# Three weight blocks of the output network decoded during attention, a ring of 25 slots, and a new order of attention's steps

## The chip, the cores and the metric

The kernel runs on one core of a Trainium2 chip. A core has five engines with queues of their own: PE (TensorE, matrix products), DVE (VectorE), ACT (ScalarE), POOL (GpSimd) and SP (SyncE, which here only issues transfers). PEld is PE's loading of stationary weights. The metric is device time in microseconds (us), less is better. The kernel before takes 501.9 us, the median of three runs from 501.25 to 503.02.

## What is computed

Three networks in a row, in fp32:

```python
scores = q @ k.T / 8                       # 4 batches x 12 heads, 448 x 448, causal
x = softmax(scores) @ v                    # -> 1792 tokens x 768
logits = x @ phi                           # 32 slots, 4 for each of 8 experts
d = softmax(logits, over tokens); c = softmax(logits, over slots)
slot_in = d.T @ x                          # 32 x 768
slot_out[e] = relu(slot_in[e] @ w1[e]) @ w2[e]      # 768 -> 1024 -> 768
y = c @ slot_out
h = y @ w_in                               # 768 -> 2048
out = (h * cos(h)) @ w_out                 # 2048 -> 768
```

The expert weights are 48 MB and must all be read once. w_in and w_out arrive as 64-bit words, 32 blocks of 768 KB, and are decoded to fp32 on the core.

## The kernel before, in words

**Attention** goes over 24 pairs of heads (4 batches x 6 pairs). The operations of a pair are small functions with short names: S0, S1, S2, Q3 are the score products of its four groups of rows (`qk_mm`, L334), sc and e the masked maximum on DVE and the exponential on ACT (`score`, L347), eps, rc and n the normalisation (L367 to L386, n on POOL unless the name ends in D or A), T0 and T1 the transposes of the probabilities for either head (`t_pair`, L399), ev0 to ev3 the copies of the transposed banks into pts (`ev_t`, L419), PV the product with v (`pv`, L424), evo the copy of x into xts (L436), X and evx the transposes of x back and their copies (L445, L452). Once in six pairs come the operations of a batch: phiA, phiB, ph4, ph5 (logits), dmax, dexp, dlg, dsum, dk, tk (the running softmax over tokens), u0, u1, ua0, ua1 (slot inputs).

The order is written out by hand: HEAD for steps 0 and 1, then ORDER once a step, TAIL from step 23. An entry ("T1", 1) in ORDER means T1 of the pair one step back. Every engine works through its own instructions in this order. `run_ops` (L634) walks it and puts loads between: when S0, S1, S2 and Q3 of a pair are out, q and k of the pair after next (`load_raw`), and in the later steps a piece of the expert weights too; after PV, the v of the pair after next.

**The ring.** `slot` (L238) gives out 26 buffers of 128 x 2048 words in turn. Attention holds seven (xk0, two for the probabilities, pts, xts, xk1, qk); the other 19 (`NPRE`, L544) take the first 19 pieces of w1 and w2, 1024 KB each, during attention. When attention is through with a slot (`FREE`, L631, seven conditions in order) the next piece goes there. xts holds x of four pairs at a time, and v of the odd pairs; x of the last pair lies in it, so its condition asks for the last X.

**The expert stream** (L822 to L862) takes the 48 pieces one after another (`next_piece`, L777). A piece that PE has used up frees its slot for a later one. Behind piece 36 the first three blocks of w_in and w_out (`NEW`) are loaded, behind piece 47 the next four. The first three are decoded (`decode`, L743) when pieces 42 to 44 are taken: an ACT pass (Prelu, L734), a DVE shift (L737) and a DVE shift with an or (L741). w_in blocks 0 and 1 go to fa, w_out block 0 to uacc.

**The output network** computes products in three fp32r terms (`back`, L949). A planner (from L1013) with costs and due times orders its operations; the first three blocks count as ready when it starts.

Of the kernel before, what the change touches and what calls it, by code (L numbers as in the profile page):

```python
# [27 lines left out]
NSLOT = 26  # L28
KP = 37
NEW = 3  # L30
# [47 lines left out]
ORDER = (  # L78
# [126 lines left out]
def moe_stack_kernel(ctx: ExitStack, tc: tile.TileContext, qk, v, cst, phi, w1, w2, w_in, w_out, out):  # L205
# [55 lines left out]
    ltr = lt[:, 0:112]  # L261
    dT = fixed.tile([128, NPB * NS], F32, name="dT")
# [35 lines left out]
    def load_piece():  # L298
        i = len(pieces)
        g, r = divmod(i, 24)  # L300
        t = slot(f"w{i}")
        if r < 12:
            SP.dma_start(t, w1[g, r // 6, r % 6])
        else:
            r -= 12
            SP.dma_start(t, w2[g, r // 4, r % 4])
        pieces.append(t)
# [13 lines left out]
    def XT(p):  # L321
        return xts[:, (p % 4) * 448:(p % 4 + 1) * 448]
# [301 lines left out]
    def all_ops():  # L624
# [7 lines left out]
            [("PV", last), ("X", last), ("phiA", 3), ("ph4", 3), ("ph5", 3)], [("u0", 3), ("PV", last - 1)], [("u1", 3), *SCORES])  # L632

    def run_ops():  # L634
# [3 lines left out]
        for op, i in all_ops():  # L638
            (PAIR if op in PAIR else BATCH)[op](i)
            done.add((op, i))  # L640
            while raws[0] < NPAIR and ok(raws[0] - 2, ("S0", "S1", "S2", "Q3")):
                load_raw(raws[0])
                raws[0] += 1
                if raws[0] > NPAIR - NPRE and len(pieces) < NPRE:
                    load_piece()
# [62 lines left out]
    def fwi(i):  # L708
        return ar[("fa", "fb")[i // 2 % 2]][:, 768 * (i % 2):768 * (i % 2) + 768]

    def it_f(j):
        kind, i = items[j]
        return fwi(i) if kind == "i" else (uacc, lt)[i % 2]
# [29 lines left out]
    def decode(j):  # L743
        dec_a(j)
        dec_l(j)
        dec_s(j)

    def up_part(c):
        f = (uacc, lt)[c % 2]
# [534 lines left out]
```

## Time and profile before

| | us |
|---|---|
| median of three runs | 501.9 |
| the profiled execution | 502.82 |
| its span, first to last instruction | 501.0 |
| PE, DVE, ACT, POOL busy | 478.5, 331.0, 307.8, 152.1 |

The page gives the busy time of each engine, the chain of waits that ended last and the costliest groups of instructions; other views give the same by stretches, lines and tiles, or in order of time. Times in the views count from the start of the span. A busy PE is not PE at its peak, since the ends of matmuls are modelled. The mean granted clock of TensorE is 0.990 of full speed.

### The profile page before, as it was taken

The page shows a single profiled execution, that of the slowest core. Times are in us where ns is not written, and L with a number is a line of the kernel's source. Part 1 is how long each engine was busy: PE and PEld are TensorE (multiplying, and loading weights), DVE is VectorE, ACT ScalarE, POOL GpSimd, SP SyncE. Part 2 cuts the span into 40 slices and gives each one's busy share as a digit, 9 for nine tenths or more (in the row PEclk, how much of TensorE's full clock was granted, in tenths as well). Part 3 has the DMA queues.
Part 4 walks back from the last instruction along what each step waited for, and adds up shares of the span by engine and source line. Part 5 has one row for each costly group of instructions (what it writes and reads, how often), then busy time and mean ns, then how long its engine had stood idle before and what let it go on. Part 6 is the DMA issues. An engine that isn't in the chain of part 4 may idle for free.

```text
span 501.0 us, 11371 instructions
## 1 busy us (share of the span) xinstructions
PE 478.5 (95%) x4329; PEld 346.2 (69%) x4329; DVE 331.0 (66%) x896; ACT 307.8 (61%) x736; POOL 152.1 (30%) x249
## 2 busy tenths in 40 slices
PE   7999999999998989879999999999999999999996
PEld 4766666666666433236877887877888888888885
DVE  4798889889885450022999888988877437336332
ACT  4898988999894110012888794858745555414452
POOL 1565555555542000000123122352421421213231
PEclk9999999999999899979999999999999999999999
DMA  6388878888867999999453545635110003023001
GB/s 204 106 285 310 292 287 295 287 294 295 289 248 259 378 423 420 419 418 418 137 178 125 190 158 217 227 108 178 61 61 2 0 2 113 14 105 118 31 1 63
DMA packets 23942, 100.38 MB, mean 200 GB/s; under 512 B 2768, under 2 KB 6352, under 8 KB 17744
## 3 DMA queue, kind: packets, MB, share of 16 engines
q1 hardware_dynamic: 23888, 99.66, 53.9%
q8 instruction: 34, 0.56, 0.5%
q14 instruction: 20, 0.16, 0.1%
HBM read 94.14 MB, written 5.51 MB: 199 GB/s over the span
## 4 chain that ended last, share of the span: by engine, by line
PE 55%; DMA 11%; DVE 3%; ACT 1%; issue 0%; SPq 0%; ACTq 0%
PE bank L954 13%; PE bank L956 13%; PE bank L955 13%; DMA w<-in_w_dram 11%; PE bank L923 3%; PE bank L984 2%; PE bank L983 2%; PE bank L985 2%; PE bank L832 2%; PE bank L884 1%; PE bank L433 1%; PE bank L542 1%; PE bank L897 1%; DVE zscr L931 1%; DVE zscr L939 0%; DVE lt L741 0%
## 5 line engine op out<-in xcount | busy, mean ns | idle before, releaser
L947 POOL TENSOR_TENSOR zg<-zscr,zg 128x512 fp32r<-128x512 f32 (+1 forms) x48 | 56.3, 1179 | 263.0 <-ACT zg L943 219.3
L954 PE MATMUL bank<-zg,zhl 128*128 128x512 f32 x282 | 112.4, 399 | 0.0
L956 PE MATMUL bank<-zg,zhl 128*128 128x512 f32 x282 | 110.2, 391 | 0.1
L955 PE MATMUL bank<-zg,zhl 128*128 128x512 f32 x282 | 110.1, 390 | 0.0
L362 ACT ACTIVATE p<-p,pst 128x192 f32<-128x192 f32 (+3 forms) x168 | 87.2, 521 | 15.3 <-DVE pst L360 14.7
L382 POOL TENSOR_SCALAR p<-p,pst 128x448 f32<-128x448 f32 (+3 forms) x123 | 66.8, 554 | 48.8 <-DVE pst L373 47.2
L931 DVE SCALAR_TENSOR_TENSOR zscr<-zscr,bank 128x512 f32<-128x512 int32 (+1 forms) x65 | 38.7, 610 | 37.4 <-ACT zscr L927 36.9
L954 PEld LDWEIGHTS bank<-zg,zhl 128*128 128x128 f32 x282 | 53.0, 188 | 12.7 <-issue 1.4
L956 PEld LDWEIGHTS bank<-zg,zhl 128*128 128x128 f32 x282 | 52.9, 188 | 11.8 <-DVE zg L947 0.4
L927 ACT ACTIVATE zscr<-bank,b_q 128x512 int32<-128x512 f32 (+1 forms) x65 | 39.4, 627 | 35.3 <-PE bank L923 33.7
L955 PEld LDWEIGHTS bank<-zg,zhl 128*128 128x128 f32 x282 | 53.1, 188 | 11.1
L344 PE MATMUL bank<-qk 64*128 64x320 f32 (+2 forms) x288 | 57.2, 467 | 0.0
L360 DVE CUSTOM_DVE_ANT_0 p<-bank,cs 128x448 f32<-128x448 f32 (+1 forms) x96 | 51.7, 553 | 5.8 <-PE bank L344 5.5
L935 ACT ACTIVATE zscr<-zscr,b_h 128x512 f32<-128x512 f32 (+1 forms) x65 | 41.6, 661 | 14.3 <-DVE zscr L931 13.3
L943 ACT ACTIVATE zg<-zscr 128x512 fp32r<-128x512 f32 (+1 forms) x65 | 36.4, 570 | 21.9 <-PE bank L955 11.4
L939 DVE TENSOR_TENSOR zscr<-bank,zscr 128x512 f32<-128x512 f32 (+1 forms) x65 | 39.0, 614 | 12.5 <-ACT zscr L935 12.5
L229 DVE COPY pts<-bank 128x512 f32<-128x512 f32 x47 | 32.1, 683 | 9.7 <-PE bank L389 9.0
L389 PE MATMUL bank<-cs,p 64*128 64x64 f32 (+1 forms) x768 | 34.7, 227 | 3.6 <-DVE p L384 2.1
L389 PEld LDWEIGHTS bank<-cs,p 64*128 64x128 f32 (+1 forms) x768 | 28.2, 133 | 12.6 <-ACT pts L227 7.1
L362 ACT ACTIVATION_READ_ACCUMULATOR p<-p,pst 128x1 f32 x168 | 31.8, 189 | 0.0
L227 ACT ACTIVATE pts<-bank 128x512 f32<-128x512 f32 x49 | 28.5, 582 | 2.3 <-PE bank L389 2.1
L734 ACT ACTIVATE zraw<-zraw 128x768 f32<-128x768 f32 x32 | 28.3, 902 | 1.6 <-DMA zraw<-in_w_out_dram 1.3
(167 smaller groups left out, 746.3 us busy)
## 6 DMA issues: line engine op xcount, KB each, us to landing
w<-in_w_dram SPq DMA_DIRECT2D x48, 1024.0 KB, 7.7
zraw<-in_w_in_dram SPq DMA_DIRECT2D x16, 768.0 KB, 4.8
zraw<-in_w_out_dram SPq DMA_DIRECT2D x16, 768.0 KB, 5.6
qk<-in_qk_dram SPq DMA_DIRECT2D x24, 480.0 KB, 3.5
xk<-in_v_dram SPq DMA_DIRECT2D x12, 256.0 KB, 3.8
out_dram<-zps SPq DMA_DIRECT2D x11, 256.0 KB, 2.1
xts<-in_v_dram SPq DMA_DIRECT2D x12, 128.0 KB, 4.0
lt<-in_v_dram SPq DMA_DIRECT2D x12, 128.0 KB, 4.1
```

The lines of the kernel that those rows point to most:

```text
L344: PE.matmul(sreg(j, c), lhsT=Q(p)[h, q0:q0 + 128], rhs=K(p)[h, 0:ln], start=True, stop=True)
L360: DVE.tensor_tensor_reduce(out=dst, in0=sb, in1=m, scale=-0.125, scalar=3.0e38, op0=ALU.add, op1=ALU.min, accum_out=st_[:, col:col + 1])
L362: return pr(f"exp{j}{c}")(lambda: ACT.activation(dst, dst, AF.Exp, bias=st_[:, col:col + 1], scale=-1.0, accum_out=st_[:, 8 + col:9 + col]))
L382: POOL.tensor_scalar(dst, dst, st_[:, 24 + col:25 + col], 0.0, op0=ALU.mult, op1=ALU.add)
L389: PE.transpose(out, src, by)
L927: ACT.activation(y_(s)[:, c].bitcast(I32), hb[:, c], AF.Identity, bias=b_q, scale=1.0 / (2.0 * math.pi))
L931: DVE.scalar_tensor_tensor(y_(s)[:, c], y_(s)[:, c].bitcast(I32), -2.0 * math.pi, hb[:, c], op0=ALU.mult, op1=ALU.add)
L935: ACT.activation(y_(s)[:, c], y_(s)[:, c], AF.Sin, bias=b_h, scale=1.0)
L947: eng.tensor_tensor(g_(s)[1][:, c], y_(s)[:, c], g_(s)[0][:, c].bitcast(F32), ALU.subtract)
L954: PE.matmul(o, lhsT=wh, rhs=gh, start=first, stop=False)
L955: PE.matmul(o, lhsT=wl, rhs=gh, start=False, stop=False)
L956: PE.matmul(o, lhsT=wh, rhs=gl, start=False, stop=last)
```

## The change

- The ring has 25 slots; 18 pieces are loaded during attention. A fixed tile, hold (128 x 2304 words), is new.
- The first three blocks of w_in and w_out are loaded into the last three of the 18 slots in steps 4 and 9, long before these take their pieces, and decoded into hold by passes that XTRA hangs behind certain operations of attention (d load, a the ACT pass, l the shift, s the shift with or). Their load and decode in the stream go. In hold they stay until the output network has used them; later hold stands in for the slot px.
- x of the last pair lies in the qk slot, and the conditions for the slots xts and qk in FREE change with it.
- HEAD, ORDER and TAIL are written anew. Norm n11 goes to DVE, n03 and n12 to POOL. The tail has one warm-up matmul (kwc) instead of seven.

The diff, with HEAD and TAIL cut to their first lines:

```diff
--- before.py
+++ after.py
@@ -25,7 +25,7 @@
 CH = ((0, 448), (128, 320), (256, 192))
 PO = (0, 448, 768)
 PW = 960
-NSLOT = 26
+NSLOT = 25
 KP = 37
 NEW = 3
 SEQ = ((0, 0, 2), (1, 0, 3), (2, 0, 4), (0, 2, 6), (1, 3, 8), (2, 4, 10), (0, 6, 13), (1, 8, 16), (2, 10, 16), (0, 13, 16), (3, 0, 16))
@@ -52,37 +52,41 @@
 LE = {1: 'D', 10: 'D', 11: 'D', 12: 'D', 13: 'D', 15: 'D', 16: 'D', 2: 'D', 23: 'D', 3: 'D', 30: 'D', 32: 'D', 39: 'D', 41: 'D', 42: 'D', 7: 'D', 9: 'D'}
 KW = 3
 HEAD = (
-    ("kwu", 1), ("S0", 0), ("sc00", 0), ("sc10", 0), ("S2", 0), ("e00", 0), ("Q3", 0), ("sc03", 0), ("S1", 0),
...
+    ("S0", 0), ("S1", 0), ("Q3", 0), ("S2", 0), ("sc00", 0), ("sc01", 0), ("sc10", 0), ("sc03", 0), ("kwu", 4),
...
+XTRA = {("e00", 4): ("d0",), ("n00", 3): ("d1",), ("sc00", 6): ("a0",), ("e01", 5): ("l0",), ("S2", 12): ("s0",),
+        ("S0", 9): ("d2",), ("n10", 10): ("a2",), ("rc1", 14): ("l2",), ("ev3D", 16): ("s2",), ("sc12", 15): ("a1",),
+        ("PV", 11): ("l1",), ("e03", 19): ("s1",)}
 TH = 2
 TT = 23
 TAIL = (
-    ("epsD1", 22), ("n03", 22), ("dsum", 2), ("S0", 23), ("e10", 22), ("e11", 22), ("Q3", 23), ("sc03", 23),
...
+    ("e01", 22), ("rc0", 22), ("evx0A", 20), ("e12", 22), ("ua0", 2), ("T1", 21), ("ev2A", 21), ("n00A", 22),
...
 ORDER = (
-    ("epsP1", 1), ("S0", 0), ("e10", 1), ("phiB", 8), ("e11", 1), ("e12", 1), ("dkc", 9), ("rc1", 1), ("phiA", 6),
-    ("Q3", 0), ("n03D", 1), ("n01", 1), ("PV", 2), ("n02", 1), ("sc03", 0), ("sc10", 0), ("u0", 9), ("u1", 11),
-    ("dsum", 12), ("e03", 0), ("T0", 1), ("dmax", 8), ("epsP2", 1), ("evo", 2), ("ua1", 12), ("S1", 0), ("sc00", 0),
-    ("rc2", 1), ("ua0", 10), ("n11", 1), ("ev1D", 1), ("n10", 1), ("X", 2), ("e00", 0), ("dlgD", 8), ("ev0A", 1),
-    ("dexp", 8), ("evx1A", 2), ("S2", 0), ("n12D", 1), ("epsP0", 0), ("T1", 1), ("dk", 8), ("sc01", 0), ("sc02", 0),
-    ("evx0D", 2), ("e01", 0), ("rc0", 0), ("tk", 8), ("ev2A", 1), ("tokc", 8), ("ev3D", 1), ("e02", 0), ("sc12", 0),
-    ("sc11", 0), ("n00", 0))
+    ("rc0", 1), ("dmax", 8), ("ua0", 12), ("dlgD", 8), ("T1", 2), ("e01", 1), ("epsP1", 1), ("S0", 0), ("S2", 0),
+    ("ev2A", 2), ("u1", 12), ("ev3D", 2), ("phiA", 6), ("e11", 1), ("evx0D", 3), ("e10", 1), ("u0", 9), ("dexp", 8),
+    ("Q3", 0), ("rc1", 1), ("ua1", 12), ("n03", 1), ("n00", 1), ("sc10", 0), ("e12", 1), ("n02", 1), ("sc03", 0),
+    ("n01", 1), ("sc12", 0), ("sc00", 0), ("sc02", 0), ("epsP2", 1), ("PV", 2), ("e03", 0), ("tk", 8), ("dk", 8),
+    ("T0", 1), ("e00", 0), ("rc2", 1), ("evo", 2), ("S1", 0), ("dsum", 9), ("X", 2), ("n11D", 1), ("n12", 1),
+    ("tokc", 8), ("ev0A", 1), ("ev1D", 1), ("sc01", 0), ("sc11", 0), ("e02", 0), ("evx1A", 2), ("dkc", 8), ("n10", 1),
+    ("epsP0", 0), ("phiB", 7))
 CFG = {'rm': 2,
         'evx': 'D',
         'evo': 'A',
@@ -259,6 +263,7 @@
     uacc = fixed.tile([128, DM], F32, name="uacc")
     lt = fixed.tile([128, DM], F32, name="lt")
     ltr = lt[:, 0:112]
+    hold = fixed.tile([128, 3 * DM], F32, name="hold")
     dT = fixed.tile([128, NPB * NS], F32, name="dT")
     dk = fixed.tile([128, 4, NS], F32, name="dk")
 
@@ -298,7 +303,7 @@
     def load_piece():
         i = len(pieces)
         g, r = divmod(i, 24)
-        t = slot(f"w{i}")
+        t = pre[i] if i < NPRE else slot(f"w{i}")
         if r < 12:
             SP.dma_start(t, w1[g, r // 6, r % 6])
         else:
@@ -319,6 +324,8 @@
         return t[:, o:o + 64]
 
     def XT(p):
+        if p == NPAIR - 1:
+            return qks[:, 1536:1984]
         return xts[:, (p % 4) * 448:(p % 4 + 1) * 448]
 
     def XK(p):
@@ -629,7 +636,22 @@
     last = NPAIR - 1
     SCORES = [(x, last) for x in ("S0", "S1", "S2", "Q3", "sc03")]
     FREE = ([("u0", 2), ("u1", 2)], [("T0", last - 1), ("T1", last - 1)], [("T0", last), ("T1", last)], [("PV", last)],
-            [("PV", last), ("X", last), ("phiA", 3), ("ph4", 3), ("ph5", 3)], [("u0", 3), ("PV", last - 1)], [("u1", 3), *SCORES])
+            [("PV", last), ("X", last - 1), ("phiA", 3), ("ph4", 3)], [("u0", 3), ("PV", last - 1)], [("u1", 3), ("X", last), ("ph5", 3), *SCORES])
+
+    pre = [slot(f"w{i}") for i in range(NPRE)]
+    early = [(pre[NPRE - 1 - j][:, 0:1536], hold[:, x:x + 768]) for j, x in enumerate((0, 1536, 768))]
+
+    def early_op(x, j):
+        src, f = (t.bitcast(I32) for t in early[j])
+        w = src.rearrange("p (n t) -> p n t", t=2)
+        if x == "d":
+            SP.dma_start(src, (w_out if j == 1 else w_in)[j // 2].bitcast(I32))
+        elif x == "a":
+            ACT.activation(w[:, :, 1].bitcast(F32), w[:, :, 1].bitcast(F32), AF.Prelu, scale=2.0 ** -112, alpha=2.0 ** 32)
+        elif x == "l":
+            DVE.tensor_scalar(w[:, :, 0], w[:, :, 0], 29, None, op0=ALU.logical_shift_right)
+        else:
+            DVE.scalar_tensor_tensor(f, w[:, :, 1], 3, w[:, :, 0], op0=ALU.logical_shift_left, op1=ALU.bitwise_or)
 
     def run_ops():
         done = set()
@@ -638,6 +660,8 @@
         for op, i in all_ops():
             (PAIR if op in PAIR else BATCH)[op](i)
             done.add((op, i))
+            for x in XTRA.get((op, i), ()):
+                early_op(x[0], int(x[1]))
             while raws[0] < NPAIR and ok(raws[0] - 2, ("S0", "S1", "S2", "Q3")):
                 load_raw(raws[0])
                 raws[0] += 1
@@ -706,11 +730,16 @@
         return ar[f"raw{j % NRAW}"][:, 0:1536]
 
     def fwi(i):
+        if i < 2:
+            return hold[:, 768 * i:768 * i + 768]
         return ar[("fa", "fb")[i // 2 % 2]][:, 768 * (i % 2):768 * (i % 2) + 768]
 
     def it_f(j):
         kind, i = items[j]
-        return fwi(i) if kind == "i" else (uacc, lt)[i % 2]
+        return fwi(i) if kind == "i" else f_o(i)
+
+    def f_o(c):
+        return (uacc, lt)[c % 2] if c else hold[:, 1536:2304]
 
     def part(blk, m):
         if blk == 0:
@@ -740,18 +769,13 @@
         fi = it_f(j).bitcast(I32)
         DVE.scalar_tensor_tensor(fi, rawv(j)[:, :, 1], 3, fi, op0=ALU.logical_shift_left, op1=ALU.bitwise_or)
 
-    def decode(j):
-        dec_a(j)
-        dec_l(j)
-        dec_s(j)
-
     def up_part(c):
-        f = (uacc, lt)[c % 2]
+        f = f_o(c)
         for t, o, m0, nm in w_cols(c, 0):
             ACT.activation(t[:, o:o + 128 * nm], f[:, 128 * m0:128 * (m0 + nm)], AF.Copy)
 
     def lo_part(c, eng):
-        f = (uacc, lt)[c % 2]
+        f = f_o(c)
         for t, o, m0, nm in w_cols(c, 1):
             m = m0
             while m < m0 + nm:
@@ -782,16 +806,12 @@
             load_piece()
             if len(pieces) == KP:
                 arena(*[f"raw{i}" for i in range(NRAW)], "fa", "fb")
-                for j in range(NEW):
-                    ld(j)
                 break
-        if len(pieces) == 48 and loaded[0] == NEW:
+        if len(pieces) == 48 and not loaded[0]:
             for j in range(NEW, NEW + NRAW):
                 ld(j)
         k = npc[0] - 46 + NEW + NEW // 2
-        if 0 <= k < NEW:
-            decode(k)
-        elif NEW <= k < NEW + NEW // 2:
+        if NEW <= k < NEW + NEW // 2:
             arena(f"hl{k - NEW}")
             up_part(k - NEW)
             lo_part(k - NEW, DVE)
@@ -862,7 +882,8 @@
                     keep_warm(2)
 
     CT = ex["CT"]
-    arena("WS", "scr", "g0", "g1", "ps", *[f"hl{i}" for i in range(NEW // 2, 12)], "ps2", "px")
+    arena("WS", "scr", "g0", "g1", "ps", *[f"hl{i}" for i in range(NEW // 2, 12)], "ps2")
+    ar["px"] = hold
     WS, scr = ar["WS"], ar["scr"]
     oT = out[0:DM * TOK[3]].rearrange("(d t) -> d t", d=DM)
 
```

## Rows read from the trace of the kernel before

**Rows 1.** The page: busy time by engine; the chain that ended last, by engine.
```profile
PE 478.5 (95%) x4329; PEld 346.2 (69%) x4329; DVE 331.0 (66%) x896; ACT 307.8 (61%) x736; POOL 152.1 (30%) x249
...
PE 55%; DMA 11%; DVE 3%; ACT 1%; issue 0%; SPq 0%; ACTq 0%
```

**Rows 2.** The chain in order of time: start, us, what (the stream's ends).
```profile
180.65 14.98 DMA w<-in_w_dram
...
234.71 1.05 PE bank L847 x16
```

**Rows 3.** Stretches: length, each engine's busy us (instructions), granted clock, DMA share, GB/s.
```profile
158.00:166.00 8.00, 6.25 (x94) 4.89 (x92) 4.81 (x19) 1.55 (x6) 0.00 (x0) 1.00 0.98 368
...
183.00:235.00 52.00, 45.05 (x554) 19.59 (x558) 7.53 (x17) 6.23 (x12) 0.00 (x0) 0.93 1.01 419
...
252.00:501.00 249.00, 244.69 (x1241) 200.74 (x1239) 164.61 (x255) 147.94 (x247) 67.32 (x54) 1.00 0.27 96
```

**Rows 4.** DMA issues by line: count, KB each, median us to landing.
```profile
w<-in_w_dram SPq DMA_DIRECT2D x48, 1024.0 KB, 7.7
zraw<-in_w_in_dram SPq DMA_DIRECT2D x16, 768.0 KB, 4.8
```

**Rows 5.** SP's issues in order of time: start, us, line (pts, xts, third block).
```profile
158.40 0.33 SPq L306 DMA_DIRECT2D w<-in_w_dram  x1
160.04 0.33 SPq L306 DMA_DIRECT2D w<-in_w_dram  x1
...
188.25 0.33 SPq L727 DMA_DIRECT2D zraw<-in_w_in_dram  x1
```

**Rows 6.** Decode lines L734, L737, L741: ns min/median/max, first and last start.
```profile
L734 ACT ACTIVATE zraw<-zraw x32: 879/899/938, 215.2 to 367.2; 128x768 f32<-128x768 f32 x32
...
L737 DVE TENSOR_SCALAR uacc<-zraw x8: 548/554/1649, 217.6 to 367.4; 128x768 int32<-128x768 int32 x8
...
L741 DVE SCALAR_TENSOR_TENSOR lt<-zraw,lt x8: 946/956/2060, 238.5 to 370.5; 128x768 int32<-128x768 int32 x8
```

**Rows 7.** Stretches, as rows 3: 18 pairs of steady attention.
```profile
26.00:136.75 110.75, 108.00 (x1645) 72.80 (x1645) 97.87 (x419) 100.53 (x334) 62.50 (x146) 1.00 0.83 296
```

**Rows 8.** PE in one step, in order of time: T0, S1, X, S2, T1, PV.
```profile
90.96 0.70 PE L389 MATMUL bank<-cs,p 64*128 64x64 f32 x16
91.50 0.76 PE L344 MATMUL bank<-qk 64*128 64x320 f32 x4
92.09 0.39 PE L448 MATMUL bank<-cs,xts 64*112 64x64 f32 x8
92.32 0.54 PE L344 MATMUL bank<-qk 64*128 64x192 f32 x4
92.98 0.73 PE L389 MATMUL bank<-cs,p 64*128 64x64 f32 x16
...
95.12 1.47 PE L433 MATMUL bank<-pts,xts 128*64 128x64 f32 x12
```

**Rows 9.** The copies of transposed banks in that step, on DVE and ACT.
```profile
91.74 0.69 DVE L229 COPY pts<-bank 128x512 f32<-128x512 f32 x1 [0.45 <-PE bank L389]
...
92.17 0.59 ACT L227 ACTIVATE pts<-bank 128x512 f32<-128x512 f32 x1
...
94.39 0.68 DVE L229 COPY pts<-bank 128x512 f32<-128x512 f32 x1
```

**Rows 10.** PE between attention and the stream, in order of time.
```profile
166.05 1.44 PE L542 MATMUL bank<-cs 128*128 128x128 f32 x6 [0.35 <-DVE phs L554]
167.42 6.45 PE L832 MATMUL bank<-w,phs 128*4 128x512 f32 x48
```

**Rows 11.** A decode pass on DVE and POOL's work beside it, in order of time.
```profile
261.29 2.06 DVE L741 SCALAR_TENSOR_TENSOR lt<-zraw,lt 128x768 int32<-128x768 int32 x1
...
259.88 2.66 POOL L947 TENSOR_TENSOR zg<-zscr,zg 128x512 fp32r<-128x512 f32 x2 [16.05 <-PE bank L923]
```

**Rows 12.** ACT's lines: one of its two table loads (the other opens the span).
```profile
L657 ACT ACT_TABLE_LOAD x1 | 1.3, 1283 | 0.0
```

37 rows, old and new, of tables (HEAD, TAIL) are left out of this document.

## The prediction

> **What bounds the kernel now.** I read the page first: PE is busy 95% of the span, but the chain of waits that ended last is PE for 55% and the transfer of the expert weights (w) for most of its 11% of DMA [rows 1]. The chain in order of time says where: from 180.65 us to 234.71 us it holds w transfers and nothing else, and then PE with the last piece (L847) [rows 2]. So there are three stages. Attention (to about 166 us) is set by its engines, the expert stream (to 234.7) by the DMA queues, and the rest by PE, which is busy for 244.69 of its last 249 us [rows 3]. What shortens the stream brings the last stage forward by as much: the chain in it is PE to the end, and its plan is left alone.
>
> In the stream the queues move 419 GB/s at a busy share of 1.01 for 52 us: they are full. Just before, from 158 to 166 us, when attention's slots come free one by one, they move 368 GB/s [rows 3].
>
> **The change, term by term**, against the profiled execution: 502.82 us, with a span of 501.0. The median of the runs is 501.9, 0.9 lower.
>
> 1. *Three blocks leave the stream.* Each is 768 KB [rows 4], issued on SP in the middle of the w pieces [rows 5]. 786,432 bytes at 419 GB/s are 1.88 us; three are 5.63 less.
>
> 2. *The ring is one slot shorter.* 18 pieces instead of 19 lie ready when attention ends; the seven slots that attention frees come at the same moments, and each takes the piece before. So one more 1024 KB piece goes through the full queue [rows 4]: 1,048,576 bytes at 419 GB/s, 2.50 more. Terms 1 and 2 make −3.1. They rest on the queue staying full: PE needs 1.05 us for a piece [rows 2] that takes 2.50 to come, so it is not late there, and the four blocks behind the last piece come forward with it. The three ACT and six DVE passes that decoded the three blocks ran in idle time of the stream; their removal is worth nothing.
>
> The Trainium skill ("DMA: Bandwidth & Descriptors", Specifications) puts the HBM limit of a core near 358 GB/s. By it the two terms would be −3.7, an estimate. The trace has 419, and that decides.
>
> 3. *The xts slot comes free earlier.* Its piece was issued at 160.04, after the last transposes of x, the piece before it at 158.40 [rows 5]. With x of the last pair in qks the two go together. The queue was 51 GB/s short of 419 for 8 us there, 0.97 us of transfer [rows 3]. Between 0 and −1.0 I take −0.5.
>
> 4. *Decode in attention.* Per block one ACT pass of 0.90 us, a DVE shift of 0.55 and a DVE shift-and-or of 0.95 [rows 6]: 7.2 for three, on engines that are close behind PE. In a steady stretch of 18 pairs (110.75 us) PE is busy 108.00, DVE 97.87, ACT 100.53 [rows 7]: per pair, DVE has 0.72 us idle and ACT 0.57. The shift now writes in place, every second word, instead of into a row of its own; I leave it at 0.55 (at worst the 0.95 of the other pass). No engine gets two passes in one step. A shift fits; an ACT pass is over by 0.33, a shift-and-or by 0.23: 1.7 in all. I let half of that reach PE, since several exponentials lie ready ahead of the transposes that need them: +0.8. Ends: 0 (all in idle time) and +7.2 (all on the path). What is late next is then T0 or T1, which wait for normalised probabilities.
>
> The three loads cost SP an issue of 0.33 us each [rows 5]. Their slots are unused, so they wait for nothing and hold back nothing. Two go out in step 4, before the first w piece, one in step 9, ahead of that step's v and the next qk; it can delay those by its own 1.88 us, and qk is wanted a pair later. I take nothing.
>
> 5. *The new order in attention.* PE's order in a step was S0, Q3, PV, T0, S1, X, S2, T1; it becomes T1, S0, S2, Q3, PV, T0, S1, X. As a cycle only S2 has moved, from between T0 and T1 to between T1 and PV. In one pair of the trace T0 starts at 90.96, S2 at 92.32, T1 at 92.98 [rows 8]. T1 overwrites the banks that T0 filled, so it follows their copies: DVE's ends at 92.43, ACT's, queued behind an exponential, at 92.76, 0.22 before T1 [rows 9]. S2's own cost I estimate from S1's, 0.59 for 320 columns [rows 8]: 0.36 for 192. Without S2 there, PE would be ready for T1 at 92.32. ACT's new order has no exponential between evo and the copy, so this should end near DVE's: T1 at 92.65, 0.33 earlier, and S2's 0.36 comes back behind it, where it covers part of PV's wait for the copy that ends at 95.07 [rows 8, 9]. I take 0. Ends: +0.36 in 22 pairs, +7.9, where ACT's copy stays as late; −3.4, where all of PE's idle time (2.75 us in 18 pairs [rows 7]) goes in 22. Of the norms, two short ones (64 and 192 columns) go from DVE to POOL and one of 320 comes back: about even.
>
> 6. *Head and tail of attention* hold the same operations in another order. Only the warm-up matmuls of the tail go from 7 to 1; three of them stand ahead of the first expert piece, 1.44 us until 167.42 [rows 10]. PE may begin the stream a little earlier or at a lower clock; with the queue as the bound neither is worth anything. I take 0, and ±1.4 for both ends.
>
> Sum: −3.1 − 0.5 + 0.8 + 0 + 0 = −2.8, or 500.0 for the profiled execution, **499.1** as a median. px in hold instead of a slot, and weights read from hold, change no instruction's size: nothing.
>
> **Rivals.**
> *A: attention gets shorter as well.* For it: PE waits in the pair above. Against it: the two cycles came out equal. Price −3.4: 495.7.
>
> *B: the decode collides with POOL.* In attention POOL is busy for 62.50 of 110.75 us [rows 7]; in the stream it is idle. One row has the price: a shift-and-or took 2.06 instead of 0.95 while POOL's subtractions ran until 262.54 [rows 11], and the longest shift took 1.65 [rows 6]. Six passes at +1.1 are +6.6; at POOL's share of 56%, 3.7; half of that on the path, 1.9: 501.0. All six on the path would be 505.7. The Trainium skill ("SBUF — State Buffer", Who interferes with whom) has the rule: DVE in a two-port mode or with two SBUF inputs and a GpSimd instruction exclude each other for a whole instruction. The row agrees.
>
> *C: slower, by the place of S2.* If ACT's copy of T0 stays late in its queue, T1 waits as now and S2 no longer fills the wait. At 0.36 a pair that is +7.9: 507.0. It decides from 2.8 / 22 = 0.13 us a pair. For it: ACT has only 0.57 us idle a pair. Against it: a wait of PV goes in exchange.
>
> *D: the moved ACT pass isn't the same pass there.* If Prelu is not in the table that the exponentials use, each of three costs two loads of 1.28 us [rows 12]: +7.7, 506.8. Against it: it ran between the sines with no load of its own.
>
> **How the numbers follow.** Forecast 0.55, with a range of its own of 497.6 to 500.6 (terms 3, 4 and 6, each off by about half of its near end); A 0.15, B 0.18, C 0.09, D 0.03. A measurement of this kernel can tell 0.3%, 1.5 us, from no change: faster is below 500.4, slower above 503.4. Faster: 0.53 of the forecast and A, 0.68. Same: the forecast's rest and B, 0.20. Slower: C and D, 0.12. The range holds the forecast, nearly all of A, and B's middle: 495.5 to 502.5, with about 0.15 left out.
>
> **What would show it.** Right: the last piece (L847) starts near 231.5 instead of 234.71; no zraw load between the w pieces on SP; about 419 GB/s still; the issues for pts and xts next to each other; attention's pairs still 6.15 us. Wrong: attention's end, or its qk issues, off by more than 2 us; DVE's early passes at 1.5 us or more beside POOL (B); T0 to PV longer than the 4.16 us of the pair above (C); a third table load (D); or the stream's end forward and the span not, which would mean that the last stage starts on something other than w.

## The result, and the profile after

The changed kernel took 496.98 us, the median of 12 runs (496.06 to 501.75), and the kernel before 501.72 (12 runs, 500.62 to 503.62): a ratio of 0.9913, with a 95% interval from 0.9897 to 0.9929, or 4.4 us less (the two medians stand 4.7 apart). Two repeats of the changed kernel on other occasions (below) gave 498.83 and 498.08. Over all its 24 runs the median is 497.9, 3.8 below before, and single runs lie between 495.9 and 501.75. The profiled execution took 496.42, with a span of 494.3.

The page of after, busy time by engine and the chain that ended last by engine [rows 1]:

```profile
PE 471.2 (95%) x4317; PEld 349.4 (71%) x4317; DVE 327.2 (66%) x876; ACT 307.3 (62%) x737; POOL 159.5 (32%) x268
...
PE 77%; DMA 12%; DVE 6%; ACT 3%; POOL 1%; issue 1%; ACTq 0%; DVEq 0%; SPq 0%
```

PE's share of the chain looks new, but it is attention that is followed back another way; the stream is where it was. The longest pieces of the chain in order of time, from the end of attention [rows 2]:

```profile
163.68 5.31 PE bank L852 x48
171.35 15.86 DMA w<-in_w_dram
187.27 20.75 DMA w<-in_w_dram
208.11 19.81 DMA w<-in_w_dram
227.96 1.05 PE bank L867 x16
```

The third transfer ends at 227.92, and the last piece (now L867) starts at 227.96 instead of 234.71. From there to the end of the span are 266.3 us in either trace (501.0 − 234.71, 494.3 − 227.96), and 266.1 to 266.5 in the traces of all the experiments below. So all of the gain lies ahead of the last piece, the last stage is as it was, and the start of the last piece measures what an edit did in its profiled execution. The two profiled executions stand 6.75 us apart there, more than the medians; the part on the clock below shows why.

Stretches of after, columns as in [rows 3] (PE, PEld, DVE, ACT, POOL busy, granted clock, DMA share, GB/s), behind attention and in the full queue:

```profile
167.00:170.00 3.00, 2.28 (x23) 0.66 (x16) 1.40 (x4) 0.97 (x2) 0.00 (x0) 1.00 0.99 412
170.00:173.00 3.00, 3.00 (x28) 0.68 (x27) 1.43 (x7) 1.11 (x2) 0.00 (x0) 1.00 1.03 434
...
183.00:197.00 14.00, 12.60 (x175) 4.81 (x179) 0.57 (x3) 0.77 (x2) 0.00 (x0) 1.00 1.01 419
```

The queue moves 419 GB/s, as before. SP's issues in order of time [rows 5]: first the pieces for pts and xts, then the slot qk with the six pieces behind it (the profile joins neighbours into one row):

```profile
155.89 0.82 SPq L311 DMA_DIRECT2D w<-in_w_dram  x2
160.93 8.40 SPq L308 DMA_DIRECT2D w<-in_w_dram  x7
```

The two go out together, as predicted, but the piece for pts itself is 2.5 us earlier than in [rows 5]. Attention has become shorter, which the forecast had at nothing. S0 of pair 2 starts at 15.52 before and 15.53 after, S0 of pair 23 at 143.10 and 140.83.

**One plain pair.** PE of before in a pair without work for the batch, from one S0 to the next:

```profile
63.18 0.97 PE L344 MATMUL bank<-qk 64*128 64x448 f32 x3
64.08 0.34 PE L338 MATMUL bank<-qk 128*64 128x64 f32 x4
64.24 2.20 PE L433 MATMUL bank<-pts,xk 128*64 128x64 f32 x20
66.48 0.70 PE L389 MATMUL bank<-cs,p 64*128 64x64 f32 x16
67.02 0.76 PE L344 MATMUL bank<-qk 64*128 64x320 f32 x4
67.61 0.39 PE L448 MATMUL bank<-cs,xts 64*112 64x64 f32 x8
67.83 0.54 PE L344 MATMUL bank<-qk 64*128 64x192 f32 x4
68.63 0.68 PE L389 MATMUL bank<-cs,p 64*128 64x64 f32 x15 [0.25 <-DVE p L384]
69.11 0.62 PE L344 MATMUL bank<-qk 64*128 64x448 f32 x1
```

PE of after in a plain pair, from T0 to the next T0 (S0 and S2 share a row, x8; PV has two):

```profile
30.01 0.70 PE L396 MATMUL bank<-cs,p 64*128 64x64 f32 x16
30.55 0.76 PE L351 MATMUL bank<-qk 64*128 64x320 f32 x4
31.15 0.39 PE L455 MATMUL bank<-cs,xts 64*112 64x64 f32 x8
31.55 0.73 PE L396 MATMUL bank<-cs,p 64*128 64x64 f32 x16
32.12 1.39 PE L351 MATMUL bank<-qk 64*128 64x448 f32 x8
33.44 0.34 PE L345 MATMUL bank<-qk 128*64 128x64 f32 x4
33.60 1.47 PE L440 MATMUL bank<-pts,xts 128*64 128x64 f32 x12
34.91 0.61 PE L440 MATMUL bank<-pts,lt 128*64 128x192 f32 x8
35.45 0.71 PE L396 MATMUL bank<-cs,p 64*128 64x64 f32 x16
```

Matmuls overlap in these rows, so read from start to start, not by durations. Of before the first matmul of S0 stands in a row ahead, at 63.09:

| from start to start, us | before | after |
|---|---|---|
| S0 and S2 (to Q3 and to T1 before) | 0.99 + 0.80 | 1.32 |
| Q3 | 0.16 | 0.16 |
| PV | 2.24 | 1.85 |
| T0, S1 | 0.54, 0.59 | 0.54, 0.60 |
| X | 0.22 | 0.40 |
| T1 | 0.48 | 0.57 |
| sum | 6.02 | 5.44 |

S0 with S2 takes 0.47 less and PV 0.39 less; X and T1 take 0.27 more. Before, T1 with S0 and Q3 alone behind it left PV to wait for the copies of T1, and S2 stood ahead of a T1 that waited in its turn. After, S2 lies between T1 and PV, and PV waits no more: its 1.85 is what its twenty matmuls take. T1's waits for ACT's copies of T0 are gone as well. This row is before's, from 26 to 137 us (total, times, longest); in after no weight load waits so there, and PE does once, for 0.3:

```profile
PEld bank L389 <- ACT pts L227: 5.7, 13, 0.5
```

One plain pair is not the whole price. The operations of the batches moved with the order as well: the 24 matmuls of u1 went from step 11 to step 12, half of phi's from step 14 to step 13. So step 11 went from 6.11 to 5.43 and step 12 from 6.29 to 7.50, and only a whole cycle of six steps can be compared: steps 10 to 15 take 37.00 before and 36.30 after, decode included. From S0(2) to S0(23) it is 127.58 before, 125.30 after.

**The early decode** by line, with mean ns (ACT pass, shift, shift with or), and ACT's two table loads:

```profile
L650 ACT ACTIVATE w<-w 128x768 f32<-128x768 f32 x3 | 2.8, 928 | 0.0
L652 DVE TENSOR_SCALAR w<-w 128x768 int32<-128x768 int32 x3 | 1.7, 553 | 0.0
L654 DVE SCALAR_TENSOR_TENSOR hold<-w 128x768 int32<-128x768 int32 x3 | 2.9, 953 | 0.0
...
L369 ACT ACT_TABLE_LOAD x1 | 1.3, 1283 | 0.7 <-PEq L1290 0.7
L681 ACT ACT_TABLE_LOAD x1 | 1.3, 1283 | 0.0
```

Each pass lasts about as long as in the stream [rows 6], the shift in place included, and there are still two table loads [rows 12].

### The profile page after: what moved, and what is told of

Its sections match the earlier page's. It is cut to its first block, busy times and chain, and to the rows that moved or that the text cites. A ratio compares the mean times of both kernels' runs of the same rounds, so it can differ in the third digit from the quotient of the medians.

```text
span 494.3 us, 11334 instructions
## 1 busy us (share of the span) xinstructions
PE 471.2 (95%) x4317; PEld 349.4 (71%) x4317; DVE 327.2 (66%) x876; ACT 307.3 (62%) x737; POOL 159.5 (32%) x268
## 4 chain that ended last, share of the span: by engine, by line
PE 77%; DMA 12%; DVE 6%; ACT 3%; POOL 1%; issue 1%; ACTq 0%; DVEq 0%; SPq 0%
PE bank L975 13%; PE bank L977 13%; PE bank L976 13%; DMA w<-in_w_dram 11%; PE bank L351 8%; PE bank L440 7%; PE bank L396 6%; PE bank L944 3%; PE bank L1005 2%; PE bank L1004 2%; PE bank L1006 2%; DVE p L367 2%; ACT p L369 1%; PE bank L852 1%; PE bank L905 1%; PE bank L465 1%
## 5 line engine op out<-in xcount | busy, mean ns | idle before, releaser
L369 ACT ACTIVATE p<-p,pst 128x320 f32<-128x320 f32 (+3 forms) x168 | 87.4, 526 | 11.5 <-DVE pst L367 11.1
L389 POOL TENSOR_SCALAR p<-p,pst 128x448 f32<-128x448 f32 (+1 forms) x140 | 73.1, 537 | 28.8 <-DVE pst L380 11.0
L351 PE MATMUL bank<-qk 64*128 64x448 f32 (+2 forms) x288 | 52.9, 464 | 0.2 <-DMA qk<-in_qk_dram 0.2
L351 PEld LDWEIGHTS bank<-qk 64*128 64x128 f32 x288 | 29.8, 191 | 6.7 <-issue 1.2
```

The costliest lines, as they stand in the source:

```text
L351: PE.matmul(sreg(j, c), lhsT=Q(p)[h, q0:q0 + 128], rhs=K(p)[h, 0:ln], start=True, stop=True)
L369: return pr(f"exp{j}{c}")(lambda: ACT.activation(dst, dst, AF.Exp, bias=st_[:, col:col + 1], scale=-1.0, accum_out=st_[:, 8 + col:9 + col]))
L389: POOL.tensor_scalar(dst, dst, st_[:, 24 + col:25 + col], 0.0, op0=ALU.mult, op1=ALU.add)
```

## The experiments

Times are medians; "before" is the kernel before on the same occasion.

| kernel | us (runs) | before | ratio, 95% |
|---|---|---|---|
| changed, repeat 1 | 498.83 (6) | 501.64 | 0.9933, 0.9906 to 0.9960 |
| changed, repeat 2 | 498.08 (6) | 501.72 | 0.9925, 0.9906 to 0.9944 |
| order alone | 500.10 (12) | 501.64 | 0.9973, 0.9956 to 0.9991 |
| all but the order | 502.80 (12) | 501.64 | 1.0018, 1.0002 to 1.0033 |
| only S2 moved | 523.45 (4) | 501.64 | 1.0432, 1.0418 to 1.0446 |
| no early decode | 497.44 (6) | 501.49 | 0.9908, 0.9884 to 0.9932 |
| loads back in the stream | 502.21 (12) | 501.49 | 1.0022, 1.0004 to 1.0039 |
| x back in xts | 497.56 (8) | 501.49 | 0.9925, 0.9900 to 0.9951 |
| warm-up matmuls back | 497.73 (7) | 501.72 | 0.9934, 0.9910 to 0.9958 |
| the same, third load earlier | 498.63 (6) | 501.72 | 0.9937, 0.9916 to 0.9958 |
| before without its warm-ups | 503.06 (12) | 501.72 | 1.0021, 1.0002 to 1.0040 |
| warm-ups in two gaps | 496.98 (6) | 501.75 | 0.9910, 0.9889 to 0.9931 |

The theory after the comparison of traces: the queue gives about 3 us, as forecast, and the order about 3 more. Its rivals are that the queue or the slots give all of it, or that S2's place alone gives the order's part.

**The changed kernel again**, as the measure for the others.

> The changed kernel again, as the measure for the others. Both theories: 0.991 of the kernel before, about 497.2 us against 501.7. If its trace again has a step of attention without batch work at 5.44 us (6.02 before), that is the order and not this one execution.

498.83, and in the second repeat 498.08. Its profiled execution (498.6) shows what after's did not: PE at half clock for 10.2 us from 160.0 on. Stretches of this repeat, columns as above:

```profile
158.00:161.00 3.00, 2.11 (x36) 1.74 (x38) 1.53 (x8) 1.55 (x6) 0.00 (x0) 0.83 0.99 399
161.00:164.00 3.00, 2.21 (x35) 1.70 (x27) 1.39 (x6) 0.00 (x0) 0.00 (x0) 0.50 1.04 415
...
167.00:170.00 3.00, 3.00 (x16) 0.45 (x12) 2.15 (x6) 0.63 (x1) 0.00 (x0) 0.50 0.90 289
```

At 167 to 170 us after had 412 GB/s at clock 1.00 and this has 289 at 0.50. I come back to it.

**The order alone**: the kernel before with HEAD, ORDER and TAIL of the changed one.

```diff
-HEAD = ...; TAIL = ...; ORDER = ...        # before's
+HEAD = ...; TAIL = ...; ORDER = ...        # the changed kernel's
```

> The kernel before with only HEAD, ORDER and TAIL of the changed one: 26 slots, three blocks still loaded and decoded in the stream. Theory O (the order itself shortens attention, by about 3.3 us over the steady steps): attention's S0 of the last pair 3 us earlier than before, time 498.0 to 499.0. Theory Q (only the queue's bytes and the earlier xts slot pay, and attention's gain in the trace of the changed kernel is chance or comes with the early loads): 501.2 to 502.2.

By the medians it is 1.5 us faster than before. In the profile S0(2) to S0(23) took 126.42, with one wait for q and k that came late:

```profile
PEld bank L345 <- DMA qk<-in_qk_dram: 1.8, 1, 1.8
```

(waits from 60 to 85 us: total, times, longest). Without it the steps are 2.9 shorter than before's 127.58. The plain ones take 5.43 to 5.44. So the order is worth about 3 us in attention by itself. It doesn't all arrive: this execution, the longest of its twelve, had the 10.2 us at half clock as well, and its last piece started at 234.68. Of the twelve, the four with a mean granted clock of 0.990 took 501.66 to 503.28, the eight above it 498.61 to 500.25.

**All but the order**: the changed kernel with before's three tables.

```diff
-HEAD = ...; TAIL = ...; ORDER = ...        # the changed kernel's
+HEAD = ...; TAIL = ...; ORDER = ...        # before's
```

> The changed kernel with HEAD, ORDER and TAIL of before; early decode, 25 slots and x of the last pair in qks stay, the early passes hang behind the same named operations. Theory O: the queue's -3.1 and -0.5 stay, the order's -3.3 goes, and the decode costs 1 to 2 us where its places were not chosen for this order: 499 to 501. Theory Q: 497 to 498, as the changed kernel.

1.1 us slower than before. The steps take 131.74, 4.2 more, in the steps with decode passes: step 6 7.02 (6.22 before), step 12 7.72 (6.29), step 16 6.83 (6.02), step 18 7.11 (6.48). The waits of attention (26 to 145 us), in all, times, longest:

```profile
ACT p L368 <- DVE pst L366: 7.8, 17, 1.0
PEld bank L395 <- ACT pts L230: 7.7, 13, 1.1
```

T1 waits for ACT's copies of T0, as in before (there 5.7 in all), and more with the passes in ACT's and DVE's queues; the waits for norms and for other copies make up the rest. −3.1 from the queue and +4.2 make +1.1, what the times show. In before's order and at these places, the decode costs more than the loads save.

**Only S2 moved**, in before: the move that the prediction saw as the whole of the new order.

```diff
-    ("epsP1", 1), ("S0", 0), ("e10", 1), ...
+    ("epsP1", 1), ("S0", 0), ("S2", 0), ("e10", 1), ...
-    ("dexp", 8), ("evx1A", 2), ("S2", 0), ("n12D", 1), ...
+    ("dexp", 8), ("evx1A", 2), ("n12D", 1), ...
```

> The kernel before with one entry of ORDER moved: S2 directly behind S0 instead of between X and T1. Theory O, that it is S2's place: PE needs less for S2 beside S0 and PV no longer waits, so 0.1 to 0.15 us a step less over 21 steps, 499 to 500. Rival C of the prediction, with ACT's copies as late as before: T1 waits and S2 fills nothing, up to +0.36 a step, 502 to 509.

4.3% slower, 6.64 a plain step. Waits from 60 to 150 us:

```profile
PEld bank L344 <- DVE pst L360: 8.4, 12, 0.8
...
PE bank L344 <- DVE pst L360: 4.8, 12, 0.5
```

S2 writes into the two banks that hold the products of S1 and S2 of the pair before, so DVE must have read them there (sc01, sc02, sc11, sc12), and in before's order sc12 and sc11 still stand at the end of the step. In one step of this trace the second half of S2 starts at 116.10, right behind sc11, which ends at 116.04. In the new ORDER sc12 and sc02 come ahead of PV, and T1 and S0 lie between sc11 and S2. DVE's order had to move with S2; moved by itself S2 costs 22 us.

**No early decode**: the nine passes are left out and hold is zero, so the output network computes with three weight blocks of zeros.

```diff
-        elif x == "a":
-            ACT.activation(...)
-        elif x == "l":
-            DVE.tensor_scalar(...)
-        else:
-            DVE.scalar_tensor_tensor(...)
+        POOL.memset(hold, 0.0)
```

> The changed kernel without the nine early decode passes (their loads stay; hold is filled with zeros once at the start, so three blocks of the output network's weights are zero). The difference to the changed kernel is what decoding in attention costs. By the trace (steps 12, 18 and 19 longer by 0.4, 0.4 and 0.2 than their like) about 1 us: 496.0 to 496.5 against 497.2. By rival B (collisions with POOL, 1.9 on the path) 495. If it costs nothing: 497.2.

497.44: no difference that the runs can tell. Step by step the trace can: steps 12, 14, 19 and 20 are 0.03, 0.11, 0.16 and 0.35 shorter than after's, 0.65 in all, the others equal (three with a late q or k aside). So in the new order the decode costs 0.65 in attention.

It also shows who pays for a collision. POOL's small additions in attention (ns min/median/max), in after and then without decode:

```profile
L376 POOL TENSOR_SCALAR pst<-pst x55: 230/230/1062, 27.4 to 135.5; 128x2 f32<-128x2 f32 x37, 128x3 f32<-128x3 f32 x18
```

```profile
L376 POOL TENSOR_SCALAR pst<-pst x55: 230/232/243, 26.7 to 135.8; 128x2 f32<-128x2 f32 x37, 128x3 f32<-128x3 f32 x18
```

The longest one of after ran beside a shift-and-or, POOL's row first and then DVE's:

```profile
119.41 1.06 POOL L376 TENSOR_SCALAR pst<-pst 128x3 f32<-128x3 f32 x1
...
119.42 0.95 DVE L654 SCALAR_TENSOR_TENSOR hold<-w 128x768 int32<-128x768 int32 x1
```

DVE kept its 0.95 and POOL went from 0.23 to 1.06. Whether the 0.16 and 0.35 of steps 19 and 20 come of this late addition was not tested.

**The three loads back** behind piece 36 in the changed kernel, unused.

```diff
                 arena(*[f"raw{i}" for i in range(NRAW)], "fa", "fb")
+                for j in range(NEW):
+                    ld(j)
+                loaded[0] = 0
                 break
```

> The changed kernel with the three 768 KB loads put back behind piece 36 of the stream, into the raw slots, where nobody uses them. Theory of the full queue: three times 1.87 us, +5.6, 502.8. If the stream's end is set by something else, or the last stage does not start on the last piece: less than +3.

502.21, which is 3.4 to 5.2 more than the three medians of the changed kernel; its last piece starts at 236.89, 6.8 behind the first repeat's, of which attention and its last slots are 1.0. From the landing of the piece in the qk slot to that of the last piece are 65.25 us here and 59.52 in the first repeat, so in the stream the loads cost 5.73, against 5.63 predicted. The transfers were not hidden; why the medians stand less than that apart is open.

**x of the last pair back in xts**, with before's conditions in FREE.

```diff
-        if p == NPAIR - 1:
-            return qks[:, 1536:1984]
...
-            [("PV", last), ("X", last - 1), ...], ..., [("u1", 3), ("X", last), ("ph5", 3), *SCORES])
+            [("PV", last), ("X", last), ...], ..., [("u1", 3), *SCORES])
```

> The changed kernel with x of the last pair back in xts, and the conditions for the slots xts and qk as before. Its piece is then issued after the last X instead of after PV, 1.5 to 2.5 us later, in a stretch where the queue is not full. Term 3 of the prediction: +0.5 (between 0 and +1.0), 497.5 to 498.2. If the queue is already behind there: 0.

497.56, inside the spread of the changed kernel. The xts piece was issued at 158.85, 1.5 behind that for pts (157.35). The last piece came at 231.46, 1.3 behind the first repeat's, with an attention 0.4 longer. The runs can't tell the third term from 0, nor from the 0.5 predicted.

**The clock at the end of attention.** The first changed execution has no stretch at half clock there, before has 3.4 us (from 166.3), and of the other profiled executions with the new tail as it is, five have 10.2 and one (loads back) 6.8. PE of the first repeat, then of after, in the same place (u0 and u1, the slot products, the first expert matmuls):

```profile
159.89 1.49 PE L536 MATMUL bank<-xk,dk 112*32 112x128 f32 x24 [0.39 <-DVE dk L513]
161.15 1.52 PE L536 MATMUL bank<-qk,dk 112*32 112x128 f32 x24
...
163.97 2.77 PE L558 MATMUL bank<-pst,uacc 128*128 128x32 f32 x12 [0.79 <-DVE pst L591]
166.67 1.89 PE L852 MATMUL bank<-w,phs 128*4 128x512 f32 x8
```

```profile
159.31 0.86 PE L536 MATMUL bank<-xk,dk 112*32 112x128 f32 x24 [0.38 <-DVE dk L513]
159.99 0.84 PE L536 MATMUL bank<-qk,dk 112*32 112x128 f32 x24
...
162.15 1.52 PE L558 MATMUL bank<-pst,uacc 128*128 128x32 f32 x12 [0.79 <-DVE pst L591]
163.61 2.76 PE L852 MATMUL bank<-w,phs 128*4 128x512 f32 x24
```

The qk slot, which waits for u1, comes at 162.76 instead of 160.93, and the first slot that PE frees in the stream at 168.62 instead of 164.71; the last piece starts at 230.12 instead of 227.96. An attention 0.6 longer is part of this, and the rest goes with the clock. Theory K, as the expectations call it, was that this costs the changed kernel time in most runs, and that the warm-up matmuls it dropped would buy it back. Four runs bear on it.

> The changed kernel a third time, beside the next three. Both theories: 0.991 to 0.993 of the kernel before, 497 to 498.5 us; in its trace either no stretch of half clock around 160 to 170 us (as in the first trace, span 494.3) or one of 10.2 us (as in the second, span 496.5).

The second repeat had half clock from 147.7 for 3.4 us and from 161.3 for 10.2 us; 498.08, last piece at 230.34. Its S0(23) stands at 140.80, where after's does, so here the whole 2.4 us by which the last piece is later come behind it.

The first edit puts eight warm-up matmuls back into the changed kernel, in two gaps and at the end of the tail:

```diff
-    ..., ("X", 23), ("dmax", 3), ("evx0A", 23), ("dlgD", 3),
+    ..., ("X", 23), ("dmax", 3), ("kwc", 3), ("evx0A", 23), ("dlgD", 3),
-    ..., ("slots", 3), ("ua1", 3), ("bs0", 3), ("bsc0", 3), ("bs1", 3), ("bsc1", 3))
+    ..., ("slots", 3), ("kwc", 2), ("ua1", 3), ("bs0", 3), ("bsc0", 3), ("bs1", 3), ("bsc1", 3), ("kwc", 3))
```

> The changed kernel with eight warm-up matmuls more at the end of the tail (three after the maximum of the logits, two after the slots' weights, three before the first expert piece), where before had seven and the change left one. Theory K (the half-clock stretch of 10.2 us, which costs the queue about 2 us there, comes from PE's idle time in the new tail): no such stretch, or one under 4 us, and 0.5 to 2 us less than the changed kernel, 495.5 to 496.8. Theory N (the clock falls there for reasons that the warm-ups don't touch, or the queue hides it): as the changed kernel, or 0.5 us more for the added PE work.

The stretch is down to 3.4 us from 164.4, the qk slot comes at 161.00, and the last piece starts at 229.25. But 497.73 is not measurably less than the changed kernel's 497.9; and the three last warm-ups stand ahead of the first expert matmul (165.42 against 163.61).

The next has the same warm-ups and one load earlier:

```diff
-        ("S0", 9): ("d2",), ...
+        ("n00", 2): ("d2",), ...
```

> The one before, and the third block's load in step 3 instead of step 9. In traces of the changed kernel q and k take 4 to 7 us to land in steps 9 to 12 (3.4 to 4.9 before), and in some PE waits for them once, 1 to 1.6 us. If the block's 768 KB behind a piece is what makes them late: no wait for qk, 0.3 to 1 us less than the run with the warm-ups alone. If the shorter steps are it, no difference.

This puts the third block's load into step 3, ahead of all w pieces, against the late q and k. No q or k was late in its profile, and 498.63 is no gain either. The early loads are not needed to make q and k late: the order alone has none of them, and its wait of 1.8 us was the longest.

The next takes the warm-ups out of the kernel before:

```diff
-    ..., ("X", 23), ("kwc", 4), ("dexp", 3),
+    ..., ("X", 23), ("dexp", 3),
-    ("bs1", 3), ("bsc1", 3), ("tokc", 3), ("kwc", 3))
+    ("bs1", 3), ("bsc1", 3), ("tokc", 3))
```

> The kernel before without its seven warm-up matmuls at the end of the tail, and nothing else. Theory K: the half-clock stretch of 3.4 us that begins at 166.3 in its trace comes earlier and lasts about 10 us, and 1 to 2.5 us are lost: 502.7 to 504.2. Theory N: 501.5, or 0.5 us less for the work saved.

Before without its seven warm-ups: 1.3 us slower by the medians, in two heaps, four runs from 500.4 to 501.3 and eight from 502.8 to 505.5. The profiled one (501.27) is of the first and had no such stretch at the border. The four had a mean granted clock of 0.992 to 0.997, the eight of 0.983 to 0.990. So warm-ups are worth something there, but not in every run.

> The changed kernel with warm-up matmuls in two gaps of its tail (three behind dmax, two behind slots) and none at the end. Theory K (the stretch at half clock at the end of attention costs time): the gaps are filled and no warm-up stands ahead of the first expert piece, so no stretch or one of 3.4 us, the first expert matmul near 165.0, the last piece near 228.0, 495.5 to 497.0 us. Rival (the stretch takes nothing that the full queue does not take back): last piece near 229, 497.0 to 498.6 us, as the changed kernel itself.

This is the kernel with warm-ups in the two gaps without the three at the end: 496.98, exactly the changed kernel's first median, and 0.9 below that over all its runs, which six runs can't tell from nothing. Its profiled execution, one of its slowest (499.06), had no stretch at the border but one of 3.4 us at 148.6: the third slot (p1) came at 155.97 instead of after's 153.65, and the last piece at 230.54; its S0(23) was 0.9 late as well. Filling the gaps doesn't reliably prevent a stretch, and one ahead of the slots comes with late slots and a late end of the stream.

The mean granted clock of every execution is on record, and it parts the 24 of the changed kernel without overlap. The eleven at 0.995 or more took 495.9 to 497.32 us (median 496.57); the thirteen at 0.993 or less took 497.9 to 501.75 (median 498.85). So 2.3 us go with the clock. That the clock alone costs them isn't shown: eighteen of the nineteen executions with warm-ups were at 0.995 or more, and their median is 497.8. The warm-ups bring back the clock, but not clearly the time.

## Why the prediction was right, and where it was wrong

The forecast, 499.1, is 2.1 above the first median and 1.2 above that of all runs; 497.9 lies in the forecast's own range, and direction and range held. The sum behind it is right in the queue (terms 1 and 2) and nearly right in the decode (4), wrong in the order (5) and the tail (6), and open in 3. That the total came so near is in part luck: the 2.9 that the order gave beyond the forecast are set off by the 1.6 that executions at a lower clock took back and by the 0.5 that the third term may not have given.

| term | predicted | the runs showed |
|---|---|---|
| 1, 2: the queue | −3.1 | −3.2 to −3.6 in the stream; loads back cost 5.73 there, 3.4 to 5.2 in the medians (5.63 predicted); 419 GB/s still |
| 3: xts earlier | −0.5 | not told from 0 (x back) |
| 4: decode | +0.8 | +0.65 in the new order; +4.2 in the old one |
| 5: order | 0 (+7.9 to −3.4) | −2.9 in attention |
| 6: tail | 0 (±1.4) | up to +2.4, in executions at half clock there |

With −3.1 for the queue and nothing for the tail the terms add up to −5.4, and the median of all runs is −3.8. The 1.6 between is where executions differ from one another: q and k late in some (0.98 us of waiting in the first repeat), and the clock at the border. The eleven executions with the higher clock have a median 5.2 below before's 501.72, close to the sum, so nearly all of the 1.6 goes with the clock.

**Terms 1 and 2 held as a mechanism.** The piece in the qk slot lands at 172.75 before and 169.65 after; from there the stream is pieces and blocks at the full queue's rate. From that landing to that of the last piece are 61.91 us before. Between executions that are alike in the clock at the border it is 61.49 for before without its warm-ups against 58.27 for after, and 63.13 for the order alone against 59.52 for the first repeat: 3.2 and 3.6 less, against 3.13 predicted. The Trainium skill's limit of about 358 GB/s for a core ("DMA: Bandwidth & Descriptors", Specifications) is exceeded here too, by the 419 of the rows.

**Term 5 is the step that failed.** The prediction read the pair at 90.96 [rows 8]. In that pair the two small transposes of tk stand between T1 and S0, and they already cover the wait of PV that S2 covers in the new order; so the gain seemed to go to and fro, and I took 0. Such a pair is one in six. In a plain pair the rows above show 0.39 of wait ahead of PV and the wait of T1 behind S2, both gone. Rival A had the right size for this term, −3.4, for a reason that only half fits: that was all of PE's idle time in 18 pairs [rows 7], but PE loses more than that in a plain pair (0.58), takes on work of other steps in a batch step, and its modelled busy time hid the difference: 108.00 of 110.75 looked like little to gain.

And "as a cycle only S2 has moved" held for the products of a pair on PE alone; the batches' products and the orders of DVE and ACT moved too. That move alone costs 22 us; for it to pay, the masked maxima of the same banks had to move ahead on DVE. Which of the other moves pay how much was not tried one by one. Rival C named the right risk (an S2 in a place where a wait takes over) at the wrong wait: not T1 behind ACT's copy, but S2 behind DVE.

**Term 6 failed in its reason.** It held that a lower clock at the start of the stream is worth nothing because the queue is the bound. At 167 to 170 us the first repeat, at half clock, moved 289 GB/s where after moved 412. PE was busy for all of these 3 us, and it freed its first slot 3.9 us later than in after, so for a while PE was the bound there. The chain of before already runs over PE and ACT from 166.05 to 180.65, ahead of the w transfers that the prediction read [rows 2].

**Term 4 was right for its sum but not by itself.** Decode and order were costed apart. In before's order the same passes cost 4.2, between the bounds of 0 and 7.2, because ACT's copies of T0 already ended late there; in the new order hardly a wait of PE on these copies is left, and the passes cost 0.65.

**Rival B**: the collision is there, but it is POOL that waits, and the decode passes on DVE kept their length. The Trainium skill says that the one that issues first takes the shared pair of ports for the whole instruction ("SBUF — State Buffer", Who interferes with whom); the rows at 119.4 agree with the exclusion. They don't tell which issued first: the two begin 0.01 us apart, and in the second repeat, where POOL takes 1.06 as well, less than that. In [rows 11] it was DVE that lost. **Rival D**: no third table load.

Of the tests named ahead, the 419 GB/s, the missing zraw loads, pts and xts together, and the two table loads came out; attention's pairs did not stay at 6.15, and the last piece came 3.5 ahead of the 231.5 named (about 1.3 in the repeats). One of the signs of being wrong that the prediction named showed as well: in the first profiled execution attention's last S0 came 2.3 us early and the qk slot 3.3, more than the 2 us allowed.

## What to carry to other kernels

Cost an edit of the order over a whole cycle of steps, not on one: the pair that the prediction read had extra work that happened to fill the gap, and a plain pair alone (0.58) would have promised 12.8 us in 22 steps, where 2.9 came. Measure from start to start, since busy time of a pipelined engine hides waits. Two edits on the same tight engines have no prices of their own: try each alone and both together. A fresh place for one instruction is worth what the queues of the other engines allow, so move their consumers with it.

## What the runs showed that was not expected

- Executions of one and the same kernel differ by what the clock does at a stage's border: PE at 1.2 instead of 2.4 GHz for 0, 3.4, 6.8 or 10.2 us, behind a series of short waits of PE of 0.4 to 0.8 us. The same 24 matmuls took 0.86 and 1.49 us. What tips it was not found, and warm-up matmuls in two of the gaps shortened it without a clear gain in the median.
- Time won in a stage can make the next thing late: with steps of 5.4 us and a 1024 KB piece in each, the queues in attention run at a share of up to 0.92 (0.83 before), and in some executions a load of q and k that usually lands in 4 to 6 us took over 7 and stopped PE:

```profile
73.25 1.35 PE L351 MATMUL bank<-qk 64*128 64x448 f32 x8 [0.98 <-DMA qk<-in_qk_dram]
```

(PE of the first repeat, in order of time.)
